# Spreading loads, moving zero rows, and moving three kinds of result stores to Pool's DMA ring in a decode backward kernel

## Chip, cores, metric

One Trainium2 chip, one core. The metric is the device time of one execution in microseconds; smaller is better. An execution can fall into a slower state. A few times by the profiler are quoted from the start of the span; the span is some 1.8 us shorter than the time.

## The reference

The kernel computes the forward result and all gradients of one decode step that adds sliding-window attention over a cache and a GeGLU feed-forward block:

```
xn  = layernorm(x)                                   # x: 4 x 1 x 512
out = x + attention(xn, k_cache, v_cache, wq, wo)    # 32 heads, 8 kv heads, window: last 1024 of 4096 rows
        + (gelu(xn @ w_gate) * (xn @ w_up)) @ w_down # F = 1792
grads of (x, k_cache, v_cache, wq, wo, w_gate, w_up, w_down) for grad_out
```

Two things matter. The gradients of the caches have the full shape 4 x 8 x 4096 x 128, and three quarters of each lie outside the window and are zero: 50.3 MB of zeros must be written. With weights, window and results 112.15 MB are moved.

## The kernel before

The 8 kv heads are worked off in 4 groups of 2 (`t` = 0 to 3). In front of them runs the feed-forward part. Finished results are cast into one pool of four buffers and stored; small pieces of such work stand in a list `bg`, and `tick(n)` takes n of them between other work.

```python
outp = ctx.enter_context(tc.tile_pool(name="outp", bufs=4))     # osb_d, osb_g, osb_o, osb_q all live here
...
    def load_w(t):                                   # weights of a group: 1 MB each
        eng = nc.gpsimd if t else nc.sync            # Pool's ring, except for group 0
        wo_t[t] = pool.tile([P, HG, D], BF16, name="wo_sb", tag="wo")
        eng.dma_start(out=wo_t[t][:], in_=wo_v[t])
        wq_t[t] = pool.tile([P, ND, CW], BF16, name="wq_sb", tag="wq")
        eng.dma_start(out=wq_t[t][:], in_=wq_v[t])
...
    def piece_q(c2, k, held):                        # dwq: rows of 2 KB
        if k == 0:
            held["osb"] = outp.tile([P, 2, GP, rep * Dh], BF16, name="osb_q", tag="o")
...
            store(nc.sync, out=out_4...)
    def piece_d(f4, i, n, held):                     # dWdown: rows of 1 KB
...
            store(nc.sync, out=out_8...)
    def piece_g(s_r, og, c, i, held):                # dWgate, dWup: rows of 3.5 KB
...
            store(nc.sync, out=og...)
...
        load_w(1)                                    # 1 MB + 1 MB
        for k in range(2):
            load_kv(1, k, 1)                         # 1 MB + 1 MB
        for t in range(NT):
...
            odq(t)
            fin(t)
            load_next(t)                             # loads of group t + 2
            tick(len(bg))
            dw(t)
        tick(2)
        zeros(4)                                     # ACT issues zero rows; more stand inside scores()
        tick(len(bg))
        zeros(2 * B * G)
```

So there are three rings, each a queue of transfers that one engine issues: ACT issues zeros (q10), SP issues all results and the loads for the start (q1), and Pool issues loads and nothing else (q0). Pool also makes P_x, the masked attention probabilities, once per group. When the P_x of a group begins tells how far compute has come.

Of the kernel before, what the change touches and what calls it, by code (L numbers as in the profile page):

```python
# [13 lines left out]
BF16 = mybir.dt.bfloat16  # L14
P = 128
# [3 lines left out]
def kernel(  # L19
# [27 lines left out]
    nc = tc.nc  # L47

    B, Sq, D = A_x.shape
# [7 lines left out]
    ND = D // P  # L57
# [4 lines left out]
    NT = G // GP  # L62
    HG = GP * rep
# [5 lines left out]
    CW = HG * Dh  # L69
# [33 lines left out]
    def store(eng, out, in_, kind, apart):  # L103

        d = eng.dma_start(out=out, in_=in_)
        for k in apart:
            tc.declare_no_dep(d.ins, group=k, reason="stores write disjoint parts of the outputs")
        tc.add_to_no_dep_group(kind, d.ins)
        return d
# [6 lines left out]
    for c0 in range(0, NF, NF // 2):  # L116
        nc.sync.dma_start(out=wd_sb[:, c0:c0 + NF // 2, :],
                          in_=B_w_down[c0 * P:(c0 + NF // 2) * P, :].rearrange("(c p) n -> p c n", p=P))
# [47 lines left out]
    for b in range(B):  # L166
        nc.vector.tensor_copy(out=sel[:, :, b * rep:(b + 1) * rep],
                              in_=ident_f[:, b * RB:b * RB + 1].unsqueeze(2).broadcast_to([P, 2 * GP, rep]))
# [69 lines left out]
    for src, dstT, adj in ((dy_b, dyT, False), (xn_b, xnT, True)):  # L238
# [4 lines left out]
        if src is dy_b:  # L243
# [3 lines left out]
                                  in_=tps[:].rearrange("p c (b r) -> p c b r", b=B)[:, :, :, 0:8])  # L247
# [22 lines left out]
    wo_v = A_wo.rearrange("(t p k) n -> t p k n", p=P, k=HG)  # L270
# [5 lines left out]

    loads = deque()

    def load_w(t):
        eng = nc.gpsimd if t else nc.sync  # L280
        pool = wpool[t % 2]
        wo_t[t] = pool.tile([P, HG, D], BF16, name="wo_sb", tag="wo")
        eng.dma_start(out=wo_t[t][:], in_=wo_v[t])
        wq_t[t] = pool.tile([P, ND, CW], BF16, name="wq_sb", tag="wq")
        eng.dma_start(out=wq_t[t][:], in_=wq_v[t])

    def load_kv(t, k, g):
        d_, src, nm = ((k_t, A_k_cache, "kb"), (v_t, A_v_cache, "vb"))[k]
        tl = kvpool[(GP * t + g) % (2 * GP)].tile([P, J, Dh], BF16, name=nm, tag=nm)
        (nc.gpsimd if GP * t + g > GP else nc.sync).dma_start(out=tl[:].rearrange("p j d -> p (j d)"),  # L290
                          in_=src[:, t * GP + g, K0:Sk, :].rearrange("b (m j) d -> m b (j d)", j=J))
        d_[(t, g)] = tl

    def load_next(t):

        if t + 2 < NT:
            load_w(t + 2)
            for k in range(2):
                for g in range(GP):
                    loads.append(lambda k=k, g=g: load_kv(t + 2, k, g))  # L300
# [94 lines left out]
    def scores(t, k, hooks):  # L395

        lf = (qm, dom)[k]
        blks = (k_t, v_t)[k]
        ps = ps_a.tile([P, WQ], FP32, name="S_ps", tag=("S", "dP")[k])
        for g in range(GP):  # L400
            for q in range(NQ):
                T_ps = ps_w.tile([P, JQ, P], BF16, name="T_ps", tag="w")
                for jj in range(JQ):
                    nc.tensor.transpose(T_ps[:, jj, :], blks[(t, g)][:, q * JQ + jj, :], ident[:])  # L404
                T_sb = tsb.tile([P, WQ, B], BF16, name="T_sb", tag="T", bufs=4)
                evac(T_sb[:].rearrange("p n b -> p (n b)"), T_ps[:].rearrange("p j m -> p (j m)"), 1024, half=True)
                s = q * GP + g
                for b in range(B):
                    nc.tensor.matmul(ps[b * RG:(b + 1) * RG, :], lhsT=lf[:, b, s * RG:(s + 1) * RG],  # L409
                                     rhs=T_sb[:, :, b], start=(g == 0 and q == 0),  # L410
                                     stop=(g == GP - 1 and q == NQ - 1), tile_position=(0, b * RG))
                for f in hooks.get(g * NQ + q, ()):
                    f()
                tick(2 if k or q % 2 else 1)
                if q == 1 and loads:
                    loads.popleft()()
                if q == 1:
                    zeros(ZN[t][GP * k + g])
        st[t][("S", "dP")[k]] = ps[:]
# [135 lines left out]
    def dw(t):  # L555

        X = st[t]["X"]

        def piece_o(g, i, held):
            if i == 0:  # L560
                held["osb"] = outp.tile([P, rep, D], BF16, name="osb_o", tag="o")
            mps = ps_w.tile([P, D], FP32, name="dwo_ps", tag="w")
            nc.tensor.matmul(mps[:], lhsT=X[:].rearrange("p h d -> p (h d)")[:, g * rep + i:CW:HG], rhs=dyz[:], start=True, stop=True)  # L563
            evac(held["osb"][:, i, :], mps[:], 512)
            if i == rep - 1:
                store(nc.sync, out=out_5[t * CW:(t + 1) * CW, :].rearrange("(p k) n -> p k n", k=HG)[
                    :, g * rep:(g + 1) * rep, :], in_=held["osb"][:], kind="rest", apart=["zeros", "rest"])

        def piece_q(c2, k, held):
            if k == 0:  # L570
                held["osb"] = outp.tile([P, 2, GP, rep * Dh], BF16, name="osb_q", tag="o")
            ci, g = k // GP, k % GP
            c = c2 * 2 + ci
            mps = ps_w.tile([P, rep * Dh], FP32, name="dwq_ps", tag="w")
            nc.tensor.matmul(mps[:], lhsT=xnz[:, c:D:ND],  # L575
                             rhs=X[:, g * rep:(g + 1) * rep, :].rearrange("p i d -> p (i d)"), start=True, stop=True)
            evac(held["osb"][:, ci, g, :], mps[:], 512)
            if k == 2 * GP - 1:
                store(nc.sync,
                      out=out_4.rearrange("(p c) j -> p c j", c=ND)[:, c2 * 2:(c2 + 1) * 2, t * CW:(t + 1) * CW],  # L580
                      in_=held["osb"][:].rearrange("p c g j -> p c (g j)"), kind="rest", apart=["zeros", "rest"])

        for g in range(GP):
            held = {}
            for i in range(rep):
                bg.append(lambda g=g, i=i, held=held: piece_o(g, i, held))
        for c2 in range(ND // 2):
            held = {}
            for k in range(2 * GP):
                bg.append(lambda c2=c2, k=k, held=held: piece_q(c2, k, held))  # L590
# [24 lines left out]


    NF4 = (NF + 3) // 4
    load_w(0)
    for k in range(2):
        for g in range(GP):  # L620
            load_kv(0, k, g)
# [84 lines left out]
    def piece_d(f4, i, n, held):  # L706
        if i == 0:
            held["osb"] = outp.tile([P, 4, D], BF16, name="osb_d", tag="o")
        mps = ps_w.tile([P, D], FP32, name="dwd_ps", tag="w")
        nc.tensor.matmul(mps[:], lhsT=a_r[:, f4, :], rhs=dym[:, i, :], start=True, stop=True)  # L710
        evac(held["osb"][:, i, :], mps[:], 512)
        if i == n - 1:
            store(nc.sync, out=out_8[4 * f4 * P:(4 * f4 + n) * P, :].rearrange("(h p) n -> p h n", p=P),
                                in_=held["osb"][:, 0:n, :], kind="rest",
                      apart=["zeros", "rest"])

    def piece_g(s_r, og, c, i, held):
        if i == 0:
            held["osb"] = outp.tile([P, NF4, 4, P], BF16, name="osb_g", tag="o")
        n = (NF - i + 3) // 4  # L720
        mps = ps_w.tile([P, NF4, P], FP32, name="dwg_ps", tag="w")
        nc.tensor.matmul(mps[:, 0:n, :].rearrange("p f d -> p (f d)"), lhsT=xnm2[i // 2][:, i % 2, c:D:ND],  # L722
                         rhs=s_r[:, 0:n, :].rearrange("p f d -> p (f d)"), start=True, stop=True)
        evac(held["osb"][:, 0:n, i, :], mps[:, 0:n, :], n * P)
        if i == 3:
            store(nc.sync, out=og.rearrange("(p c) f -> p c f", c=ND)[:, c, :],
                                in_=held["osb"][:].rearrange("p f i d -> p (f i d)")[:, 0:F], kind="rest",
                      apart=["zeros", "rest"])

# [33 lines left out]
    with tc.tile_pool(name="stage", bufs=4, reuse_waits="tile") as stage, \  # L763
            tc.tile_pool(name="wodd", bufs=1, reuse_waits="tile") as wodd:
        wpool.append(wodd)
        kvpool.append(wodd)
        load_w(1)
        for k in range(2):
            load_kv(1, k, 1)
        for t in range(NT):  # L770
            if t == 0:
                pre(t, {})
            masks(t)
            scores(t, 0, {})
            zeros(2 if t == 0 else 0)
            scores(t, 1, softmax(t))
            d1, d2 = softmax_d(t)
            zeros(4 if t == NT - 1 else 0)
            if t + 1 < NT:
                pre(t + 1, {0: [d1], 2: [d2]})  # L780
            else:
                tick(2)
                d1()
                tick(6)
                d2()
                tick(2)
            odq(t)
            fin(t)
            load_next(t)
            tick(len(bg))  # L790
            dw(t)
        tick(2)
        zeros(4)
        tick(len(bg))
        zeros(2 * B * G)

# [65 lines left out]
```

## Time and profile before

| | before |
|---|---|
| time, median of 6 runs | 281.11 us (280.98 to 281.59) |
| span of the profiled run | 279.9 us |
| last vector copy of the result dx | 269.1 us |
| most DMA engines end | 274.7 us |
| last store's last packet | 278.4 us |

The times in the last three rows come from the instruction and packet records. "Most engines end" is the last moment at which at least six of the 16 DMA engines were busy. One more view is needed, the DMA issues: output and input, issuing engine, count, KB of each, and the median time from issue to landing in us.

```profile
out_dram<-osb_q SPq DMA_DIRECT2D x8, 512.0 KB, 13.6
out_dram<-osb_g SPq DMA_DIRECT2D x8, 448.0 KB, 15.8
...
wo_sb<-in_A_wo_dram POOLq DMA_DIRECT2D x3, 1024.0 KB, 11.7
wq_sb<-in_A_wq_dram POOLq DMA_DIRECT2D x3, 1024.0 KB, 21.9
...
out_dram<-osb_d SPq DMA_DIRECT2D x3, 512.0 KB, 9.4
```

The reader is to see that every result store is SP's, and that loads of groups 1 to 3 are Pool's.

### The profile page before, as it was taken

Reading aid. Unit: us, or ns where it says so; the run is one execution under the profiler, and the core shown is the slowest. Engines: PE = TensorE matmul, PEld = TensorE weight load, DVE = VectorE, ACT = ScalarE, POOL = GpSimd, SP = SyncE. Lnnn points to the kernel's source line nnn. Section 1 sums busy time; section 2 is a strip of 40 time slices with the busy share of each in tenths; the row PEclk is TensorE's granted clock in tenths of the full one; section 3 lists DMA queues with packets and bytes.
Section 4 is the critical chain, followed back from the end, with each engine's and each line's share of the span. In section 5 each row is a group of like instructions: output and inputs, shape, how many; then the busy total and the mean of one; then the engine's idle time right before and its main releaser. Section 6 shows DMA issues by size and latency. Waiting matters only on the chain.

```text
span 279.9 us, 7186 instructions
## 1 busy us (share of the span) xinstructions
PE 215.6 (77%) x3126; PEld 140.7 (50%) x3132; DVE 158.9 (57%) x336; ACT 115.3 (41%) x214; POOL 56.0 (20%) x56
## 2 busy tenths in 40 slices
PE   1868986978669869897799897778989769789700
PEld 0856864645346645454466654445665435255300
DVE  6955744645446655563657554547766444577740
ACT  1321733454335245543342553446245435714600
POOL 3890003230200334102001550010142020020000
PEclk9975979899986977997959979999999997898975
DMA  7999999999999999999999999999999999998992
GB/s 233 448 390 429 427 404 393 409 411 417 417 426 427 424 426 409 370 423 422 431 423 419 316 417 423 432 419 427 419 422 393 424 422 421 419 428 351 396 410 114
DMA packets 19440, 112.15 MB, mean 401 GB/s; under 512 B 1473, under 2 KB 5073, under 8 KB 10449
## 3 DMA queue, kind: packets, MB, share of 16 engines
q10 hardware_dynamic: 4416, 50.34, 42.8%
q1 hardware_dynamic: 12304, 44.58, 39.3%
q0 software_dynamic: 2688, 16.78, 15.4%
q8 instruction: 24, 0.39, 0.5%
q14 instruction: 8, 0.06, 0.1%
HBM read 30.68 MB, written 81.01 MB: 399 GB/s over the span
## 4 chain that ended last, share of the span: by engine, by line
PE 56%; DVE 21%; DMA 11%; issue 4%; ACT 2%; POOL 2%; ACTq 0%; DVEq 0%
PE kv_ps L544 11%; PE T_ps L404 9%; DVE T_sb L101 6%; PE S_ps L409 6%; DMA out_dram<-osb_d 6%; DMA out_dram<-osb_g 5%; PE dwo_ps L563 3%; PE acc_ps L213 3%; PE wgT_ps L749 3%; PE wqT_ps L602 3%; PE od_ps L516 3%; PE woT_ps L341 2%; POOL P_x L424 2%; PE pT_ps L435 2%; PE dwq_ps L575 2%
## 5 line engine op out<-in xcount | busy, mean ns | idle before, releaser
L101 DVE COPY T_sb<-T_ps 128x1024 bf16<-128x1024 bf16 x64 | 43.9, 690 | 44.6 <-PE T_ps L404 44.2
L99 ACT CAST stg_dv<-kv_ps 128x512 bf16<-128x512 f32 x57 | 30.4, 592 | 30.4 <-PE kv_ps L544 30.4
L99 ACT CAST stg_dk<-kv_ps 128x512 bf16<-128x512 f32 x40 | 22.2, 588 | 40.3 <-PE kv_ps L544 26.8
L544 PE MATMUL kv_ps<-domr,P_x 128*128 128x512 bf16 x63 | 23.4, 446 | 5.4 <-POOL P_x L424 4.8
L544 PE MATMUL kv_ps<-qmr,dS_x 128*128 128x512 bf16 x60 | 22.3, 459 | 1.8 <-DVE dS_x L424 1.4
L389 POOL TENSOR_TENSOR domr<-r,msk 128x512 bf16<-128x512 bf16 x8 | 8.2, 1040 | 75.1 <-DVE r L382 75.1
L404 PE MATMUL T_ps<-ident,kb 128*128 128x128 bf16 x256 | 22.0, 226 | 0.0
L404 PEld LDWEIGHTS <-kb 128*128 128x128 bf16 x256 | 17.3, 102 | 9.2 <-issue 6.7
L99 ACT CAST osb_g<-dwg_ps 128x512 bf16<-128x512 f32 (+1 forms) x28 | 14.3, 538 | 17.9 <-PE dwg_ps L722 8.0
L404 PE MATMUL T_ps<-ident,vb 128*128 128x128 bf16 x256 | 21.4, 227 | 0.1
L99 ACT CAST osb_o<-dwo_ps 128x512 bf16<-128x512 f32 x25 | 14.6, 586 | 15.3 <-PE dwo_ps L563 14.3
L404 PEld LDWEIGHTS <-vb 128*128 128x128 bf16 x256 | 16.5, 102 | 6.8 <-issue 4.7
L424 POOL TENSOR_TENSOR P_x<-P_b,bmsk 128x1024 bf16<-128x1024 bf16 x4 | 7.6, 1891 | 57.9 <-ACT P_b L472 57.9
L409 PE MATMUL S_ps<-T_sb,dom 128*32 128x256 bf16 x128 | 12.7, 387 | 8.0 <-DVE T_sb L101 7.5
L99 ACT CAST osb_q<-dwq_ps 128x512 bf16<-128x512 f32 x25 | 13.9, 590 | 9.6 <-PE dwq_ps L575 7.5
L101 DVE CAST stg_dk<-kv_ps 128x512 bf16<-128x512 f32 x24 | 16.1, 685 | 2.3 <-PE kv_ps L544 2.2
L409 PE MATMUL S_ps<-T_sb,qm 128*32 128x256 bf16 x128 | 13.1, 389 | 5.1 <-DVE T_sb L101 5.1
L101 DVE COPY woT<-woT_ps 128x1024 bf16<-128x1024 bf16 x16 | 11.0, 689 | 10.2 <-PE woT_ps L341 10.2
L101 DVE COPY wqT<-wqT_ps 128x1024 bf16<-128x1024 bf16 x16 | 11.0, 688 | 6.1 <-PE wqT_ps L602 6.1
L341 PE MATMUL woT_ps<-ident,wo_sb 128*128 128x128 bf16 x128 | 12.3, 249 | 2.7 <-DVE stg_dv L101 1.9
L341 PEld LDWEIGHTS <-wo_sb 128*128 128x128 bf16 x128 | 10.5, 114 | 7.1 <-issue 6.2
L409 PEld LDWEIGHTS <-dom 128*32 128x32 bf16 x128 | 5.3, 93 | 17.5 <-issue 15.7
(214 smaller groups left out, 404.8 us busy)
## 6 DMA issues: line engine op xcount, KB each, us to landing
out_dram<-ztile ACTq DMA_DIRECT2D x13, 3072.0 KB, 19.7
out_dram<-ztile ACTq DMA_DIRECT2D x6, 1536.0 KB, 18.9
out_dram<-stg_dv SPq DMA_DIRECT2D x8, 1024.0 KB, 19.8
out_dram<-stg_dk SPq DMA_DIRECT2D x8, 1024.0 KB, 12.2
kb<-in_A_k_cache_dram POOLq DMA_DIRECT2D x5, 1024.0 KB, 20.4
vb<-in_A_v_cache_dram POOLq DMA_DIRECT2D x5, 1024.0 KB, 25.6
out_dram<-osb_o SPq DMA_DIRECT2D x8, 512.0 KB, 14.5
out_dram<-osb_q SPq DMA_DIRECT2D x8, 512.0 KB, 13.6
```

The source lines that it names most:

```text
L99: last.append(nc.scalar.copy(out=out, in_=in_))
L101: return nc.vector.tensor_copy(out=out, in_=in_)
L213: nc.tensor.matmul(ps[:, c, :], lhsT=lf(c), rhs=rhs, start=(k == 0), stop=(k == len(terms) - 1))
L341: nc.tensor.transpose(wT_ps[:, i, c, :], wo_sb[:, 2 * h2 + i, c * P:(c + 1) * P], ident[:])
L404: nc.tensor.transpose(T_ps[:, jj, :], blks[(t, g)][:, q * JQ + jj, :], ident[:])
L409: nc.tensor.matmul(ps[b * RG:(b + 1) * RG, :], lhsT=lf[:, b, s * RG:(s + 1) * RG], rhs=T_sb[:, :, b], start=(g == 0 and q == 0), stop=(g = ...
L424: eng.tensor_tensor(out=dst[:].rearrange("p j (m b) -> p (j m) b", b=B), in0=src[:].unsqueeze(2).broadcast_to([P, WQ, B]), in1=bmsk[:].uns ...
L516: nc.tensor.matmul(od_ps[r0:r0 + rep * B, 0, :], lhsT=pT[:, j % JQ, (j // JQ) * GP + g:P:NS], rhs=blks[(t, g)][:, j, :], start=(j == 0), s ...
L544: nc.tensor.matmul(mps[:].rearrange("p q d -> p (q d)"), lhsT=src[:, jj, :], rhs=mr[:, g].rearrange("p q d -> p (q d)"), start=True, stop= ...
L563: nc.tensor.matmul(mps[:], lhsT=X[:].rearrange("p h d -> p (h d)")[:, g * rep + i:CW:HG], rhs=dyz[:], start=True, stop=True)
L602: nc.tensor.transpose(wT_ps[:, i, c, :], wq_sb[:, c, h * Dh:(h + 1) * Dh], ident[:])
L749: nc.tensor.transpose(wT_ps[:, i, c, :], wsb[:, c, fc * P:(fc + 1) * P], ident[:])
```

## The change

Its intent: (1) put the loads of a group into a list and pop them one by one, so that they don't burst; (2) let Pool issue the stores of dwq (but for the last group), dWdown, dWgate and dWup, because Pool's ring joins short rows into longer packets (2 KB rows of wq go as packets of 4,096 B, see the prediction); (3) issue some zero rows at the ends of groups, where the DMA engines were idle.

```diff
-    def load_w(t):
+    def load_w(t, k):                  # k = 0: wo, k = 1: wq
...
         if t + 2 < NT:
-            load_w(t + 2)
+            for k in range(2):
+                loads.append(lambda k=k: load_w(t + 2, k))
...
-                if q == 1 and loads:
+                if (q == 1 or (k, q) == (0, 3)) and loads:
                     loads.popleft()()
...
-                store(nc.sync,                                        # osb_q
+                store(nc.gpsimd if t + 1 < NT else nc.sync,
...
-            store(nc.sync, out=out_8[...                              # osb_d
+            store(nc.gpsimd, out=out_8[...
-            store(nc.sync, out=og...                                  # osb_g
+            store(nc.gpsimd, out=og...
...
-        load_w(1)
         for k in range(2):
-            load_kv(1, k, 1)
+            loads.append(lambda k=k: load_w(1, k))
+        for k in range(2):
+            loads.append(lambda k=k: load_kv(1, k, 1))
...
             odq(t)
+            zeros(2 if t == NT - 1 else min(t, 1))
             fin(t)
...
-        zeros(4)
+        zeros(2)
```

More of the change, by code (lines that the diff above doesn't have):

```diff
@@ L277 @@
     loads = deque()
-    def load_w(t):
+    def load_w(t, k):
         eng = nc.gpsimd if t else nc.sync
         pool = wpool[t % 2]
-        wo_t[t] = pool.tile([P, HG, D], BF16, name="wo_sb", tag="wo")
-        eng.dma_start(out=wo_t[t][:], in_=wo_v[t])
-        wq_t[t] = pool.tile([P, ND, CW], BF16, name="wq_sb", tag="wq")
-        eng.dma_start(out=wq_t[t][:], in_=wq_v[t])
+        if k == 0:
+            wo_t[t] = pool.tile([P, HG, D], BF16, name="wo_sb", tag="wo")
+            eng.dma_start(out=wo_t[t][:], in_=wo_v[t])
+        else:
+            wq_t[t] = pool.tile([P, ND, CW], BF16, name="wq_sb", tag="wq")
+            eng.dma_start(out=wq_t[t][:], in_=wq_v[t])
     def load_kv(t, k, g):
@@ L617 @@
     NF4 = (NF + 3) // 4
-    load_w(0)
+    for k in range(2):
+        load_w(0, k)
     for k in range(2):
@@ L712, in piece_d @@
         if i == n - 1:
-            store(nc.sync, out=out_8[4 * f4 * P:(4 * f4 + n) * P, :].rearrange("(h p) n -> p h n", p=P),
+            store(nc.gpsimd, out=out_8[4 * f4 * P:(4 * f4 + n) * P, :].rearrange("(h p) n -> p h n", p=P),
                                 in_=held["osb"][:, 0:n, :], kind="rest",
@@ L725, in piece_g @@
         if i == 3:
-            store(nc.sync, out=og.rearrange("(p c) f -> p c f", c=ND)[:, c, :],
+            store(nc.gpsimd, out=og.rearrange("(p c) f -> p c f", c=ND)[:, c, :],
                                 in_=held["osb"][:].rearrange("p f i d -> p (f i d)")[:, 0:F], kind="rest",
@@ L766 @@
         kvpool.append(wodd)
-        load_w(1)
         for k in range(2):
-            load_kv(1, k, 1)
+            loads.append(lambda k=k: load_w(1, k))
+        for k in range(2):
+            loads.append(lambda k=k: load_kv(1, k, 1))
         for t in range(NT):
```

## The prediction

> **What bounds the kernel now.** I began with the page: its slices, its queues and its chain.
>
> ```profile
> DMA  7999999999999999999999999999999999998992
> GB/s 233 448 390 429 427 404 393 409 411 417 417 426 427 424 426 409 370 423 422 431 423 419 316 417 423 432 419 427 419 422 393 424 422 421 419 428 351 396 410 114
> ...
> q10 hardware_dynamic: 4416, 50.34, 42.8%
> q1 hardware_dynamic: 12304, 44.58, 39.3%
> q0 software_dynamic: 2688, 16.78, 15.4%
> ...
> PE 56%; DVE 21%; DMA 11%; issue 4%; ACT 2%; POOL 2%; ACTq 0%; DVEq 0%
> ```
>
> The reader is to see that the 16 DMA engines are full in 37 of 40 slices. q10 carries the zeros (issued by ACT), q1 what SP issues, q0 what Pool issues; with instruction fetches they add to 98% of the span. The chain of waits names TensorE first, but read in order of time it ends with the last vector copy at 269.1 us; the span ends at 279.9. The last 9 to 10 us are a queue draining. So compute has that much slack and bytes set the end: 112.15 MB at the 420 to 430 GB/s of a good slice would be 261 to 267 us.
>
> Next I cut the time into the stretches where the GB/s line dips, with the busy time of the engines and the DMA share (last two columns):
>
> ```profile
> 154.50:157.00 2.50, 1.77 (x20) 1.26 (x19) 1.38 (x2) 1.57 (x4) 2.48 (x3) 1.00 0.85 298
> 157.00:160.00 3.00, 2.71 (x47) 2.01 (x45) 2.08 (x4) 2.14 (x5) 0.71 (x2) 1.00 0.99 287
> 211.00:213.00 2.00, 2.00 (x23) 1.09 (x20) 1.64 (x3) 1.62 (x4) 1.91 (x2) 1.00 0.78 324
> ...
> 257.00:259.50 2.50, 2.50 (x7) 0.97 (x6) 2.19 (x4) 1.70 (x4) 0.00 (x0) 0.50 0.34 136
> ```
>
> Two kinds of loss are here. Idle engines at the ends of groups: 0.15 x 2.5 + 0.22 x 2 + 0.66 x 2.5 = 2.5 us. And slow packets: at 157 to 160 the share is full but only 287 GB/s move. Third, the last stretch of the queue view:
>
> ```profile
> DMA packets 41, 0.09 MB, mean 18 GB/s; under 512 B 3, under 2 KB 3, under 8 KB 41
> ## 3 DMA queue, kind: packets, MB, share of 16 engines
> q1 hardware_dynamic: 41, 0.09, 4.5%
> ```
>
> That is 274.8 to 279.9 us. 0.045 x 16 x 5.1 us = 3.7 us of engine time, spread over 3.7 us: one engine alone works off its share while 15 have ended. The same lag is in the landings of every late store (15 of 16 completions together, the last 3.8 us later; near 248 us it is 11 us). So the end is set by one lagging engine, not by the mean.
>
> **What the Trainium skill says.** "Perfetto Trace Analysis", section What "DMA-bound" means, lists "specific DMA engines" as one of the things that bind; the lag just shown agrees. "Runtime: NRT & Kernel Launch", Instruction fetch mechanics, says that instructions stream in 16 KiB blocks by DMA; the trace has 24 packets of 16,384 B of some 0.93 us each on q8, 22 us of engine time, enough to make a few engines late, though the records do not name the engine. "DMA: Bandwidth & Descriptors", SWDGE vs HWDGE vs iDMA, gives Pool's packets as 4096 B at best, of up to 64 descriptors. The trace agrees: a wq load has rows of 2 KB, and SP's one goes as 512 packets of 2048 B, each of Pool's three as 256 of 4096 B. The same page, Queues, rings and completion order, says that an engine takes turns between queues packet by packet. The trace agrees: SP's 1 KB packets run at 188 per 0.5 us alone, and at about 10 beside 8 KB packets of Pool and 12 KB packets of zeros.
>
> **The change part by part.** The diff alone misleads here; comparing the order of instructions on each engine, TensorE's order is the same but for two transposes. The scheduler hoists Pool's loads, so of the "spreading" little survives: at the end of group 0, wq moves behind the two qmr multiplies; at the end of group 1, one kb, wo and wq move behind domr or qmr. Worth: near nothing, perhaps 0.3 us in the slow stretches.
>
> *Short rows joined.* What a packet costs:
>
> ```profile
> q1 hardware_dynamic: 753, 0.75, 106.6%
> ...
> q1 hardware_dynamic: 395, 0.79, 101.6%
> ```
>
> The first line is 41.2 to 43.2 us (osb_d, 1 KB rows): 1.066 x 16 x 2 us / 753 = 45 ns. The second is 272.2 to 274.2 us (osb_q, 2 KB): 82 ns. The packet records give medians of 46, 84, 140, 159, 309 and 460 ns for 1, 2, 3.5, 4, 8 and 12 KB: some 9 ns fixed plus bytes at 27 B/ns. Moved to Pool and joined:
> - osb_d, 1792 rows of 1 KB: 1792 x 46 = 82.4 us of engine; as 448 packets of 4 KB, 448 x 159 = 71.2. Over 16 engines 0.70 us saved.
> - osb_q of three groups, 6 stores x 256 rows of 2 KB: 1536 x 84 = 129.0, as 768 x 159 = 122.1: 0.43 us.
> - osb_g, 3.5 KB rows: two do not fit in 4 KB, so I expect nothing.
>
> That is 1.1 us on every engine, the lagging one too. The zeros beside osb_d lose another 0.7 us at 35 to 56 us (12 KB packets over 460 ns); fewer small packets may give back half: 0.35.
>
> *Zeros moved.* One row (0.79 MB, 1.9 us of all engines at 420 GB/s) is now issued at the end of groups 1 and 2 each, and two rows at about 248 instead of four at 258. This puts work exactly where the engines idle: up to 2.5 us of the mean engine. But the lagging engine was 8 us behind at 216 and 11 at 248, so in the gaps at 211 and 257 it was working; it gains only what it idled near 155, at most 0.4 us. This is my main choice: I count 0.3 of the 2.5 us for the end.
>
> *Pool's slow packets.* Against 309 ns, q0's packets lost 3.0 us of 16 engines in total: 1.3 us at 154 to 161 and 0.8 at 112 to 119, where Pool's queue was nearly alone, and almost nothing beside zeros and stores. With a zero row running into 155 I take 0.9 us back; wq after qmr at 112 gains little. The new stores (2,240 packets) may show the same 20 ns extra that Pool's loads average, 2,240 x 20 / 16 = 2.8 us at worst; they run mostly beside zeros, so I take 0.2.
>
> Sum: 1.1 + 0.35 + 0.3 + 0.3 + 0.9 - 0.2 = 2.75 us, and 281.1 - 2.75 is about **278.3 us**.
>
> **Rivals.**
> *The mean engine sets the end.* Then all of 2.5 us idle time counts, and the sum is near 5 us: 276. For it: engines with more backlog could already be caught up by then; against: the single engine at the end.
> *Pool's queue becomes a wait for compute.* Before, ACT waited for buffers of osb in these pieces of the chain:
>
> ```profile
> 42.74 15.72 DMA out_dram<-osb_d
> ...
> 60.67 14.93 DMA out_dram<-osb_g
> ```
>
> Now osb_d no longer starves behind bigger packets, and its last landing should move from 58.5 to about 47. But osb_g stands in Pool's ring behind 4 MB of loads, where on SP it had a ring of its own. From 44 to about 62 us engines move 7.5 MB, 2.9 of it zeros and 4.6 osb_d and loads; then beside zeros Pool gets 8/(8+12) of 420 GB/s, 168, so 0.4 MB of loads and four osb_g (1.8 MB) need 13 us, until 75, which is where the second wait ended before (75.6). P_x also stands behind six osb_g stores on Pool, and behind two osb_q stores later, which before were issued only 1.5 to 1.7 us ahead of it. A delay of 3 us is plausible and vanishes in the 9 us of slack; beyond 7 us it would set the end, 280 to 283.
> *The bytes are hidden anyway.* If the lagging engine's load is mostly fetches and Pool packets, joining still helps it, since each store puts 1/16 on every engine. So no change at all is unlikely.
>
> **Range and chances.** The sure part is 1.1 us, the rest between -1 and +4. So 8 in 10: 275.2 to 280.6. Faster by over 2% needs below 275.5, the mean-engine rival with everything else going well: 0.13. Slower by over 2% needs Pool to stall compute by over 14 us: 0.02. Within 2%: 0.85.
>
> **What would show it.** Joining: q0 holds about 1,200 more 4 KB packets and q1 has 1,792 fewer of 1 KB and 1,536 fewer of 2 KB. Zeros: share 0.95 or more in the slices near 155, 212 and 257, yet a last engine more than 3.8 us behind the others. Pool: q0 packets under 320 ns at the end of group 1. Early phase: the two long DMA waits of the chain still ending near 75 us. Wrong, if the last stretch has no lone engine, if compute ends after the drain, or if q0's packets for the stores are 1 or 2 KB.

## The result

| | before | after |
|---|---|---|
| time, median of 6 runs | 281.11 (280.98 to 281.59) | 283.34 (282.91 to 283.82) |
| span of the profiled run | 279.9 | 281.5 |
| most DMA engines end | 274.7 | 274.2 |
| last store's last packet | 278.4 | 279.6 |
| packet work per engine, at the median of each size, without fetches and 4-byte packets | 266.1 | 264.7 |

The ratio is 1.0077, with a 95% interval of 1.0064 to 1.0090. A ratio is the mean time of one kernel's fast runs over that of the other's in the same rounds, so it isn't quite the ratio of the medians in the table. The change is within 2%, but it is slower, and outside the range of the prediction.

These lines of the page of the changed kernel answer to those of before (slices, queues, chain by engine):

```profile
DMA  7999999999999989999999999999999999999980
GB/s 234 447 392 429 423 420 413 364 404 406 424 406 430 415 356 400 364 420 424 425 426 424 382 403 429 427 419 423 428 426 418 425 429 424 429 424 423 423 327 28
...
q10 hardware_dynamic: 4448, 50.34, 42.7%
q1 hardware_dynamic: 7664, 35.92, 31.1%
q0 software_dynamic: 4704, 25.43, 22.6%
...
PE 45%; DMA 24%; DVE 18%; issue 4%; ACT 3%; POOL 2%; ACTq 0%; DVEq 0%; POOLq 0%
```

q1 lost 12304 - 7664 = 4,640 packets and q0 gained only 2,016: rows were joined. Two dips of before are filled: slice 23 rose from 316 to 382 GB/s, slice 37 from 351 to 423. But slices 15 to 17 (98 to 120 us) now carry 356, 400 and 364 (before 426, 409 and 370), and DMA has risen from 11% to 24% of the chain. The same view of stretches as in the prediction, at the old gaps and at the new ones (DMA share and GB/s are the last two columns):

```profile
98.00:105.00 7.00, 6.40 (x194) 4.77 (x191) 4.48 (x12) 1.90 (x4) 4.08 (x4) 1.00 0.86 347
112.00:119.00 7.00, 6.22 (x64) 3.94 (x61) 4.34 (x7) 3.46 (x6) 3.89 (x5) 0.88 0.96 357
154.50:157.00 2.50, 1.54 (x21) 1.15 (x19) 1.84 (x5) 1.01 (x2) 2.17 (x2) 1.00 1.02 424
...
211.00:213.00 2.00, 2.00 (x63) 1.67 (x61) 0.35 (x2) 0.24 (x1) 0.00 (x0) 0.92 0.99 412
257.00:259.50 2.50, 2.50 (x54) 1.67 (x51) 1.29 (x4) 0.59 (x1) 0.00 (x0) 0.51 0.99 415
```

In the kernel before, the first of these stretches had:

```profile
98.00:105.00 7.00, 4.72 (x37) 3.39 (x38) 3.52 (x7) 2.92 (x6) 2.46 (x3) 0.76 1.01 421
```

The zeros filled the three old gaps (0.85, 0.78 and 0.34 became 0.99 or more), and a new gap opened at 98 to 105 us (by the packet records at 103 to 105). A smaller one opened at 66 to 69; the stretch around it, before and after:

```profile
63.00:70.00 7.00, 5.69 (x60) 3.65 (x61) 3.67 (x10) 3.10 (x8) 0.14 (x1) 1.00 1.02 416
...
63.00:70.00 7.00, 2.84 (x20) 1.29 (x19) 1.14 (x3) 1.55 (x3) 0.44 (x1) 0.50 0.96 400
```

In the chain of waits of the changed kernel (start, duration, what), the two early waits of 15.7 and 14.9 us have become one:

```profile
46.43 19.99 DMA out_dram<-osb_g
```

The landings in the trace tell what it waited behind:

```
issued by Pool     issued   last of 16 engines landed
osb_d (4th)         42.58     52.7
wo, group 1         43.28     56.6
wq, group 1         43.86     59.8
kb, group 1         44.60     62.2
vb, group 1         45.14     65.3
osb_g (1st)         46.43     66.4
```

Each entry of Pool's ring lands after the one ahead of it. The first osb_g store lands 1.2 us after the last of 4 MB of loads, 20.0 us after its issue. The pool of result buffers has four; the cast of the next result waits for that one.

The durations of the chain run from the issue of a store to its landing. How long ACT itself stood still is in the list of waits (us in total, times, longest), two lines of before and one of after:

```profile
ACT osb_g L99 <- DMA out_dram<-osb_g: 6.3, 4, 3.6
ACT osb_g L99 <- DMA out_dram<-osb_d: 3.4, 2, 2.8
...
ACT osb_g L99 <- DMA out_dram<-osb_g: 9.0, 1, 9.0
```

The sum is about the same, but after the change it is one wait, from 57.6 to 66.5 us, and all of it lies before P_x of group 0. Start of P_x, from 69.9 before to 76.9 after (first and last of the four groups):

```profile
L424 POOL TENSOR_TENSOR P_x<-P_b,bmsk x4: 1888/1891/1895, 69.9 to 229.4; 128x1024 bf16<-128x1024 bf16 x4
...
L427 POOL TENSOR_TENSOR P_x<-P_b,bmsk x4: 1882/1882/1887, 76.9 to 233.1; 128x1024 bf16<-128x1024 bf16 x4
```

ACT issues its next zeros in the same stretch, at 66.6 us instead of 61.1, and SP its first store of a cache gradient (stg_dv) at 93.6 instead of 87.3.

### The profile page after: what moved, and what is told of

Read it like the earlier page. It is cut to its first block, busy times and chain, and to the rows that moved or that the text cites. A ratio compares the mean times of both kernels' runs of the same rounds, so it can differ in the third digit from the quotient of the medians.

```text
span 281.5 us, 7191 instructions
## 1 busy us (share of the span) xinstructions
PE 212.4 (75%) x3132; PEld 137.6 (49%) x3132; DVE 159.9 (57%) x336; ACT 115.0 (41%) x214; POOL 67.8 (24%) x74
## 3 DMA queue, kind: packets, MB, share of 16 engines
q1 hardware_dynamic: 7664, 35.92, 31.1%
## 4 chain that ended last, share of the span: by engine, by line
PE 45%; DMA 24%; DVE 18%; issue 4%; ACT 3%; POOL 2%; ACTq 0%; DVEq 0%; POOLq 0%
DMA out_dram<-osb_q 17%; PE kv_ps L547 7%; PE T_ps L407 7%; DMA out_dram<-osb_g 7%; PE S_ps L412 5%; DVE T_sb L101 5%; PE dwo_ps L566 3%; PE wgT_ps L753 3%; PE acc_ps L213 2%; PE woT_ps L344 2%; PE od_ps L519 2%; PE wqT_ps L605 2%; PE dwg_ps L726 2%; POOL P_x L427 1%; ACT osb_q L99 1%
## 5 line engine op out<-in xcount | busy, mean ns | idle before, releaser
L547 PE MATMUL kv_ps<-domr,P_x 128*128 128x512 bf16 x64 | 22.3, 422 | 5.4 <-POOL P_x L427 4.8
L547 PE MATMUL kv_ps<-qmr,dS_x 128*128 128x512 bf16 x64 | 21.2, 408 | 3.0 <-DVE dS_x L427 1.4
L407 PE MATMUL T_ps<-ident,kb 128*128 128x128 bf16 x256 | 22.8, 231 | 0.0
L407 PE MATMUL T_ps<-ident,vb 128*128 128x128 bf16 x256 | 22.3, 233 | 0.0
L99 ACT CAST osb_o<-dwo_ps 128x512 bf16<-128x512 f32 x25 | 14.6, 587 | 16.5 <-PE dwo_ps L566 15.7
L532 POOL TENSOR_TENSOR od_x<-od_r,hmsk 128x1024 bf16<-128x1024 bf16 x4 | 7.6, 1899 | 36.0 <-DVE od_r L523 36.0
L412 PEld LDWEIGHTS <-qm 128*32 128x32 bf16 x128 | 4.4, 93 | 20.6 <-issue 19.1
L566 PE MATMUL dwo_ps<-dyz,od_x 128*128 128x512 bf16 x32 | 14.1, 488 | 0.0
L105 POOL DMA_DIRECT2D out_dram<-osb_q x6 | 4.4, 735 | 39.2 <-ACT osb_q L99 18.7
L101 DVE COPY wgT<-wgT_ps 128x1024 bf16<-128x1024 bf16 x14 | 9.7, 692 | 7.2 <-PE wgT_ps L753 7.2
L344 PE MATMUL woT_ps<-ident,wo_sb 128*128 128x128 bf16 x128 | 11.4, 236 | 2.7 <-DVE stg_dv L101 1.9
## 6 DMA issues: line engine op xcount, KB each, us to landing
out_dram<-ztile ACTq DMA_DIRECT2D x7, 1536.0 KB, 13.3
out_dram<-osb_g POOLq DMA_DIRECT2D x8, 448.0 KB, 10.5
```

What stands on the lines that cost most here:

```text
L99: last.append(nc.scalar.copy(out=out, in_=in_))
L101: return nc.vector.tensor_copy(out=out, in_=in_)
L344: nc.tensor.transpose(wT_ps[:, i, c, :], wo_sb[:, 2 * h2 + i, c * P:(c + 1) * P], ident[:])
L407: nc.tensor.transpose(T_ps[:, jj, :], blks[(t, g)][:, q * JQ + jj, :], ident[:])
L412: nc.tensor.matmul(ps[b * RG:(b + 1) * RG, :], lhsT=lf[:, b, s * RG:(s + 1) * RG], rhs=T_sb[:, :, b], start=(g == 0 and q == 0), stop=(g = ...
L532: nc.gpsimd.tensor_tensor(out=X[:], in0=rows[:].unsqueeze(1).broadcast_to([P, HG, Dh]), in1=hmsk[:].unsqueeze(2).broadcast_to([P, HG, Dh]) ...
```

## The experiments

Theories after the first look. **E (early stall)**: osb_g stands behind the loads of group 1 in Pool's ring; compute is late, ACT issues zeros and SP stores late, and the DMA queues run dry. **Q**: the dwq stores land late in Pool's ring (one issued at 180.23 had its last landing at 229.2). **T (tail)**: at the end SP waited 4.5 and 4.0 us for landings of zeros before it could issue the last dwq store and dx. **Lone engine**: the last DMA engine, made late by instruction fetches, sets the end. Three other quantities from the packet records are used below: the mean idle time of the 16 engines in the stretches 60 to 150 us and 200 to 250 us, and the end of most engines against the last packet.

### One part undone (on the changed kernel)

**a_gsp**, osb_g back on SP:

```diff
-            store(nc.gpsimd, out=og...
+            store(nc.sync, out=og...
```

> The changed kernel with the eight osb_g stores back on SP (osb_d, osb_q on Pool, zeros and loads as changed). Theory E (early stall: osb_g waits in Pool's ring behind 4 MB of loads, a buffer wait of 20 us at 46 us, compute late by some 5 us at 100 us, DMA engines starved at 68 to 70 and 103 to 105 us by 1.3 us in the mean): the stall shrinks to what it was before (two waits of 15 us ending near 75), P_x of group 0 back near 70 us, both dips gone, time 281.3 to 282.0. Theory T (tail: the zeros moved forward leave the end unfilled and SP waits for slow zero landings) and theory Q (osb_q behind loads): time stays at 282.8 to 283.8.

Measured: 283.36 us in the three fast runs (282.24 to 284.29; a fourth, slow one took 286.71), ratio to before 1.0048 (1.0016 to 1.0080). As E says, P_x of group 0 came at 66.6 us (76.9 in the changed kernel) and the idle time of 60 to 150 us fell from 1.68 to 0.00. But the time did not come back. A second wait took its place; TensorE's waits, the chain and the stretch after it:

```profile
PE woT_ps L344 <- DMA wo_sb<-in_A_wo_dram: 13.3, 1, 13.3
...
158.37 38.66 DMA wo_sb<-in_A_wo_dram
...
205.00:217.00 12.00, 9.73 (x228) 6.63 (x226) 8.84 (x18) 4.27 (x9) 3.93 (x3) 1.00 0.60 248
```

Here the load waits behind stores: wo of group 3, issued by Pool at 158.4 us, stands behind dwq stores that Pool issued at 115.6 and 119.5 and that landed at 161 to 168. Its median landing is 183.6, its last 197.0. TensorE waits 13.3 us, and the DMA engines idle 8.6 us between 200 and 250. So the early part of E is shown, but undoing osb_g alone does not answer what it costs.

**a_qsp**, osb_q back on SP:

```diff
-                store(nc.gpsimd if t + 1 < NT else nc.sync,
+                store(nc.sync,
```

> The changed kernel with all osb_q stores back on SP. Theory Q (the osb_q stores of groups 0 to 2 stand in Pool's ring behind up to 3 MB of loads, the second of group 1 landed 49 us after its issue and held a buffer of group 2's pieces at 224 to 229 us; P_x of group 3 is 3.7 us later than before): P_x of group 3 1 to 3 us earlier, time 281.5 to 282.3, in spite of losing 0.43 us of joined rows. E and T: 283.3 to 284.0 (the lost joining, nothing else).

Measured: 283.35 us (281.36 to 285.03), 1.0065 (1.0013 to 1.0116). The runs scatter, but there is no sign of a gain: P_x of group 3, which Q wanted 1 to 3 us earlier, came at 233.8 us (233.1 in the changed kernel). Q is not the cause by itself.

**a_zold**, zeros as before:

```diff
             odq(t)
-            zeros(2 if t == NT - 1 else min(t, 1))
...
-        zeros(2)
+        zeros(4)
```

> The changed kernel with the zeros as before (four rows at 258 us, none at the group ends). Theory T: SP's last store and dx_b no longer wait 4.5 and 4.0 us for slow zero landings, dx_b issued within 1 us of its vector copy, time 281.5 to 282.5. E and Q: the idle of 2 to 2.5 us of the mean engine near 257 returns; if the last engine sets the end, time stays 283.0 to 284.0; if the mean engine does, 285.

Measured: 282.89 us (282.08 to 285.96), 1.0071 (1.0013 to 1.0130). The ratio is that of the changed kernel, so nothing speaks for T. But the edit doesn't settle it: in the profiled run, the slowest of the four, SP still waited 5.2 us for a landing of zeros before the last dwq store. Against T speaks b_z below, where the moved zeros alone cost nothing.

**a_lold**, loads as before:

```diff
-                loads.append(lambda k=k: load_w(t + 2, k))
+                load_w(t + 2, k)
-                if (q == 1 or (k, q) == (0, 3)) and loads:
+                if q == 1 and loads:
-            loads.append(lambda k=k: load_w(1, k))
+            load_w(1, k)
```

> The changed kernel with the loads issued as before (weights together at the group's end, one pop a step). In Pool's order only wq moves ahead of qmr in group 0, and wo/wq ahead of one domr in group 1. All theories E, T, Q: 283.0 to 283.7, within 0.3 us of the changed kernel. If the spreading itself costs time (loads later, DMA engines starved at 112 to 115 us, 0.3 us): 282.6 to 283.0.

Measured: 283.34 us (282.55 to 284.34), 1.0069 (1.0041 to 1.0097). The spreading of loads is neutral.

### One part alone (on the kernel before)

The edits are the matching lines of the change, so they are named only. **b_g**, osb_g on Pool:

> The kernel before with only the eight osb_g stores on Pool. Theory E: the stores stand behind 4 MB of loads, a buffer wait near 20 us, engines starved near 68 and 104 us by over 1 us in the mean: 282 to 283.5. If the ring is not the matter: 281.0 to 281.5 (packets of 7 KB join two rows, worth 0.26 us).

Measured: 285.24 us (283.09 to 286.46), 1.0109 (1.0063 to 1.0156). This part alone costs more than the whole change, and more than the 282 to 283.5 that theory E had named. The chain has the same wait, and the engines ran dry after it (0.70 of the DMA share, and TensorE nearly idle):

```profile
46.88 21.71 DMA out_dram<-osb_g
...
63.00:70.00 7.00, 0.68 (x5) 0.11 (x4) 0.14 (x1) 1.23 (x3) 0.00 (x0) 0.66 0.70 295
```

**b_d**, osb_d on Pool:

> The kernel before with only the four osb_d stores on Pool. Packet work of the mean engine falls by 0.70 us. If joined rows pay wherever they are, and the osb_d stores stand in Pool's ring before the loads: 280.0 to 280.7, 0.4 to 1.1 us below the kernel before. If stores on Pool cost in themselves (Pool's packets slow one engine): 281.5 or more.

Measured: 281.98 us (281.87 to 282.27), 1.0022 (1.0004 to 1.0041). Packet work fell by 0.7 us per engine, as worked out in the prediction. Compute ended 4 us earlier and most engines 2 us earlier, at 272.7, but the last packet stayed at 278.4, the same as before. The time lies in the range that the expectation gave to the rival, that stores on Pool slow one engine; but the kernel before took 281.64 in these rounds, so that range tells little. The rival is not excluded.

**b_q**, osb_q of groups 0 to 2 on Pool:

> The kernel before with only osb_q of groups 0 to 2 on Pool. Theory Q (the stores queue behind loads and hold buffers): 281.7 to 283. If joined rows simply pay: 280.4 to 280.9 (0.43 us of packet work).

Measured: 280.85 us (280.24 to 282.15), 0.9985 (0.9953 to 1.0017). TensorE waited 4.5 us for wq of group 3, and the engines idled 4.0 us between 200 and 250, yet it is not slower.

**b_z**, zeros moved:

> The kernel before with only the zeros moved to the group ends. If the mean engine sets the end: the idle of 2.5 us at 155, 212 and 257 us is filled and the time falls by 1.5 to 2.5 us, to 278.7 to 279.7. If a lone engine sets it: the 15 others end 2 us earlier, the lone one as before, its lag grows from 3.7 to nearly 6 us, time 280.7 to 281.4. If the moved zeros make SP wait for slow landings at the end (theory T): 281.5 to 283.

Measured: 281.00 us (280.83 to 281.76), 0.9989 (0.9969 to 1.0009). Most engines now end at 270.4, 4.3 us earlier than before, and the time stays. The last stretch shows why:

```profile
270.50:278.00 7.50, 0.00 (x0) 0.00 (x0) 0.00 (x0) 0.00 (x0) 0.00 (x0) 0.50 0.07 30
```

0.07 x 16 = 1.1 engines busy over 7.5 us: one engine works alone to 277.8. Filling the gaps helped 15 engines.

**b_l**, loads alone:

> The kernel before with only the loads spread. Pool's order changes at one or two places (wq behind qmr). If harmless: 281.0 to 281.7. If later loads starve the engines or make TensorE wait for weights: 282 or more.

Measured: 281.58 us (281.26 to 281.61), 1.0007 (0.9985 to 1.0028). Neutral.

### What the lone engine is made of

**f_few** is the kernel before with 1,536 TensorE instructions left out. Its results are wrong; the DMA bytes stay but for the instruction fetches. The core of the edit:

```diff
-            for c in range(ND):
+            for c in range(1):
...
-        for j in range(J):
+        for j in range(J // 4):
...
-  ... for k in range(HG)]
+  ... for k in range(2)]
```

> The kernel before with 1,536 fewer instructions on TensorE (a quarter of the steps of the odq products, two of eight terms of the two sums, one of four of do_ps): wrong results on purpose. Bytes, stores and loads are the same. Theory F (the instruction fetches of TensorE, 24 packets of 0.93 us, each holding one DMA engine, make the lone last engine late): 18 packets on q8, the last engine's lag at the end falls from 3.7 us to below 1.5, time 277 to 279. If the lone engine is late for another reason: lag 3 to 4.5 us, time 280.5 to 281.5, although compute ends earlier.

Measured: 278.69 us (277.79 to 280.07), 0.9907 (0.9861 to 0.9952). The fetch queue falls from 24 to 18 packets:

```profile
q8 instruction: 18, 0.29, 0.4%
```

Most engines end at 273.7 and the last at 275.9: the gap falls from 3.7 to 2.2 us, although the engines idled 5.1 us between 200 and 250. That is a little more than the bound I had put on the gap; the time lies where the fetch theory put it.

**a_few** is the same edit on the changed kernel, also wrong.

> The changed kernel with 1,536 TensorE instructions fewer, wrong on purpose. Fetch theory: 18 fetch packets instead of 24, the gap between the end of most engines and the last one falls from about 6 us to under 3.5, and the time is 2 to 3.5 us below the changed kernel's 283.3, so 279.8 to 281.3. Rival, the lone engine has another cause: the gap stays at 5 to 6 us and the time at 282.5 or more.

Measured: 280.10 us (279.48 to 280.86), 0.9974 (0.9947 to 1.0001), 3.2 us under the changed kernel. The gap between most engines and the last falls from 5.4 to 2.4 us (273.3 and 275.7). This fits, but it is not a clean test: with less TensorE work the queues no longer ran dry early either (0.16 us of idle time instead of 1.68 between 60 and 150), in spite of a first osb_g wait of 19.6 us.

In every kernel where I looked, during nearly each fetch packet of some 0.93 us the other queues keep 15.2 engines busy instead of 16.2 (transfers overlap a little, so a full set counts over 16): a fetch takes one engine away. Which engine it is the records do not tell.

**z12 and z8** were to take work off the lone engine: two of the last four zero rows of the kernel before are read from 24 or from 8 partitions, so that only 12 or 8 engines share them. The rule meant in the expectation is that of the Trainium skill, "DMA: Bandwidth & Descriptors", Why a DMA increments its semaphore by 16 and not by 1; that the lowest-numbered engines are taken is the page's word, no run here shows it.

> The kernel before with two of the last four rows of zeros written from 24 instead of 64 partitions, so that by the skill's rule 12 of the 16 DMA engines carry them, the lowest-numbered. If the lone last engine is one of the upper four it is spared 3.7 us: lag gone, time 278.7 to 279.7 (the twelve others get 1.2 us more). If it is one of the lower twelve: it gets 1.2 us more, time 282.0 to 282.8. If a lone engine does not set the end: 281.0 to 281.6.

> As before, with the two rows written from 8 partitions, so by 8 engines, the lowest-numbered. These get 3.7 us more, the upper eight 3.7 us less. If the lone engine is one of the upper eight: lower ones now end last, near 278.5, time 281 to 281.8, with eight engines at the end instead of one. If it is one of the lower eight: it ends near 282, time 284 to 285.

Measured: 286.23 us (285.99 to 288.51), 1.0193, and 304.07 us (303.80 to 304.44), 1.0809. The counts of 12 and 8 busy engines are in the records, but the 8 KB packets read from so few partitions took 641 and 1,251 ns instead of 309. That cost drowned the question; the tests say nothing on the lone engine.

### The place in Pool's ring

**e_swap** is the changed kernel with the loads of group 1 issued by SP, so that osb_g has nothing ahead of it but osb_d:

```diff
-        eng = nc.gpsimd if t else nc.sync
+        eng = nc.gpsimd if t > 1 else nc.sync
...
-        (nc.gpsimd if GP * t + g > GP else nc.sync).dma_start(
+        (nc.gpsimd if GP * t + g > GP + 1 else nc.sync).dma_start(
```

> The changed kernel with the loads of group 1 (wo, wq, kb, vb of the second head) issued by SP and no longer by Pool, so that osb_g stands behind nothing but osb_d in Pool's ring. Place-in-the-ring theory: the first osb_g store lands within 8 us of its issue (20.0 us in the changed kernel), the third softmax-gradient product P_x of group 0 ends before 71 us (76.9), the engines do not run empty at 68 to 70 and 103 to 105 us, the 7,168 B packets stay, and the time is 278.5 to 281. Rival, Pool's ring as such is slow for these stores: the first store still needs 15 us or more and the time is 282.5 to 284. A third outcome: early compute is repaired as in a_gsp, but a weight of group 3 comes late behind dwq stores in Pool's ring, TensorE waits over 5 us for it between 200 and 215 us, and the time is 282 to 284.

Measured: 286.52 us (285.32 to 287.36), 1.0198 (1.0161 to 1.0235). The third outcome, and worse than named. The early stall is gone: the first osb_g store landed 10.7 us after its issue (20.0 in the changed kernel, 8 expected), P_x came at 67.9, and the early gaps are closed. But Pool's ring still holds dwq stores ahead of the weights of group 3:

```profile
PE woT_ps L344 <- DMA wo_sb<-in_A_wo_dram: 13.5, 1, 13.5
...
157.17 41.22 DMA wo_sb<-in_A_wo_dram
...
205.00:217.00 12.00, 9.68 (x241) 6.44 (x240) 8.95 (x17) 3.79 (x7) 3.49 (x3) 1.00 0.61 249
```

**e_swap2** takes this conflict out as well: as e_swap, with the dwq stores on SP and the loads popped as before. Pool still issues osb_d and osb_g.

> As e_swap, with the dwq stores back on SP and the loads popped as in the kernel before; so Pool's ring has osb_d, osb_g and the loads of groups 2 and 3 only. Place-in-the-ring theory: P_x of group 0 ends before 71 us, no weight of group 3 comes late (TensorE waits under 2 us for wo), time 278.5 to 280.5. Rival, Pool's ring as such: 282.5 to 284.

Measured: 281.35 us (280.79 to 281.81), 1.0018 (0.9995 to 1.0042). The first store landed after 10.5 us, P_x came at 67.3, TensorE did not wait for wo or wq of group 3 (last landings at 176.5 and 168.0), and the stretch that had run dry is full:

```profile
63.00:70.00 7.00, 5.09 (x54) 3.32 (x55) 3.38 (x7) 3.97 (x9) 2.96 (x3) 1.00 1.03 431
```

The time is above the range by 0.85 us: nothing is gained, which I put down to the lone engine; but the loss is gone. Against b_g (1.0109) the difference is the loads ahead of osb_g and parts that cost about 0.2% or less (b_d, b_z, b_zd). So the loss comes from the place in the ring, and not from Pool's ring as such.

**b_zq**, zeros moved and osb_q on Pool, the two parts that had been under 1 alone:

> The kernel before with two parts of the change only: zeros moved, dwq stores of groups 0 to 2 on Pool. If their effects add (b_z 0.9989, b_q 0.9985): ratio 0.997, 280.3 to 280.9. If the late weight of b_q (TensorE waits 4 us or more for wq near 200 us) is worse with zeros in the way: 281.5 to 283.

Measured: 283.05 us (281.80 to 283.48), 1.0070 (1.0043 to 1.0098). They don't add; the second outcome holds. In the profiled run, which was the fastest of the four by 1.1 us, TensorE waited 5.7 us for wo of group 3; what made the other three slower has no trace.

**b_zd**, zeros moved and osb_d on Pool, what is left of the change when both ring conflicts are out:

> The kernel before with two parts of the change only: zeros moved, dWdown stores (osb_d) on Pool. No ring conflict is left (osb_g and dwq on SP). Lone-engine theory: most engines end near 269 to 271 us, the last one at 277 to 278.5 as in b_z and b_d, and the time is within 0.3% of before, 280.3 to 282. Rival, the saved 0.7 us and the filled gaps reach the end once the conflicts are gone: 278.0 to 279.8.

Measured: 281.58 us (281.43 to 281.76), 1.0011 (0.9980 to 1.0041). The last packet came at 278.0 and the time is that of before, as the lone engine says. Most engines ended at 275.6 and not near 270, a miss: they idled 4.8 us between 200 and 217, for which I found no single wait.

### All runs side by side

Idle times are means over 16 engines, in us; the last two columns are the end of most engines and of the last store's packets. They are those of each kernel's one profiled run, which is not always a typical one: it was the fastest in b_zq and the slowest in a_zold, a_lold and b_g. z12 and z8 are left out.

| kernel | ratio to before | idle 60-150 | idle 200-250 | most end | last |
|---|---|---|---|---|---|
| before | 1 | 0.08 | 0.43 | 274.7 | 278.4 |
| b_z | 0.9989 | 0.00 | 0.02 | 270.4 | 277.8 |
| b_q | 0.9985 | 0.00 | 4.03 | 276.8 | 278.1 |
| b_l | 1.0007 | 0.00 | 0.47 | 272.4 | 278.3 |
| b_zd | 1.0011 | 0.00 | 4.84 | 275.6 | 278.0 |
| e_swap2 | 1.0018 | 0.00 | 3.20 | 275.1 | 278.0 |
| b_d | 1.0022 | 0.00 | 0.09 | 272.7 | 278.4 |
| b_zq | 1.0070 | 0.18 | 3.75 | 275.0 | 278.3 |
| after | 1.0077 | 1.68 | 0.00 | 274.2 | 279.6 |
| a_qsp | 1.0065 | 1.30 | 0.37 | 274.7 | 279.7 |
| a_lold | 1.0069 | 1.09 | 0.08 | 274.5 | 280.6 |
| a_zold | 1.0071 | 1.75 | 0.08 | 276.5 | 282.1 |
| b_g | 1.0109 | 3.22 | 0.00 | 277.7 | 283.2 |
| a_gsp | 1.0048 | 0.00 | 8.64 | 279.9 | 281.0 |
| e_swap | 1.0198 | 0.00 | 9.00 | 281.3 | 281.9 |
| f_few | 0.9907 | 0.00 | 5.14 | 273.7 | 275.9 |
| a_few | 0.9974 | 0.16 | 0.32 | 273.3 | 275.7 |

The table reads in three blocks. Where the engines did not run dry before 150 us, the last packet comes at 277.8 to 278.4, whatever most engines did (270.4 to 276.8) and with up to 4.8 us of late idle time. Where they ran dry early, it comes at 279.6 or later. Where they idled 8.6 us or more late, it comes at 281.0 or later, and then most engines end close to it. Only the two kernels with fewer fetches, and less compute, came under 277. The ratio of b_zq (1.0070) is out of line with its last packet, for its other three runs were slower than the profiled one.

It stays open why an early gap goes with a later end and one of 5 us near 210 does not. One could think that the lone engine falls behind gradually and so has no backlog to work on in an early gap. The landings do not bear that out. In the kernel before, the last of 16 landings came 2.6 us after the median for a load issued at 106.4 us, but already 9.3 us for the next, issued at 106.9; then 6.9 us for one issued at 160.7 and 3.8 us for the last stores. In the middle of the kernel several of the 16 are late, not one: 4 of 16 by 5.9 to 10.6 us for a store issued at 238.4.

## Why the prediction was wrong

**Joined rows: right in size, worth nothing at the end.** Packet work fell by 1.39 us per engine (1.13 predicted). The 0.26 us more is osb_g: the prediction said two rows of 3.5 KB do not fit in 4 KB, and the trace has 512 packets of 7,168 B, two rows each. But of the 1.1 us credited to "every engine, the lagging one too", b_d shows none at the lone engine: 278.4 before and with it.

**Zeros: right.** The three gaps are filled, and the lone engine stayed later than 3.8 us behind the others (5.4). The main choice, that the lone engine and not the mean sets the end, is shown by b_z. What the prediction read from the landings, "15 of 16 completions together", holds for stores issued from 258 us on only; earlier several were late, as told above.

**Slow packets: right in place, lost elsewhere.** The 0.9 us credited to Pool's packets did come where it was seen: at 154 to 161 us their time over the median of each size fell from 1.3 to 0.3 us per engine (the 8 KB packets there still took 417 ns, not under 320). But at 42 to 70 us, in the middle of which Pool had the engines nearly to itself during ACT's wait, it grew from 0.4 to 0.7, and at 161 to 168 from 0.1 to 0.4. In total only 0.3 us remained (3.05 to 2.75). The 0.35 us for the zeros beside osb_d did not come: over the whole span the loss of zero packets rose from 1.70 to 2.31.

**Loads: right.** Neutral in b_l and a_lold.

**The step that failed** is the rival "Pool's queue becomes a wait for compute", which was sized as vanishing. Its mechanism was named rightly: osb_g behind 4 MB of loads. What was wrong is the event that was watched. The prediction compared the end of the second wait (75.6 before, 75 worked out) and found no delay. Four osb_g had in fact landed even sooner, by 69.7, for the sum counted zeros beside them that ACT, itself waiting, had not yet issued. But in the kernel before P_x of group 0 came at 69.9, ahead of the end of the second wait, so it can't have hung on that; it hangs on what comes before. P_x follows the end of the first wait, or the landing of the first osb_g store, by 9.7 to 11.4 us in these kernels (in e_swap and e_swap2 ACT had no need to wait for that store: its next cast came at 58.9 and 58.2 us, released by TensorE):

| kernel | first wait ends, or first osb_g landed | P_x, group 0 |
|---|---|---|
| before | 58.5 (wait for osb_d) | 69.9 |
| after | 66.4 | 76.9 |
| b_g | 68.6 | 79.1 |
| e_swap | 58.2 | 67.9 |
| e_swap2 | 57.3 | 67.3 |

So compute was 7.0 us late, which is just the bound that the prediction had set ("beyond 7 us it would set the end, 280 to 283"). It did not set the end in the way written there: dx was ready at 270.9 (269.1 before), before most engines ended. The second mistake is the word slack. That compute ended later did no harm by itself, but compute issues the zeros and produces the stores, so a delay of 7 us emptied the queues at 66 to 69 and 103 to 105 us (with smaller gaps 1.68 us of idle time against 0.08). The last packet came 1.2 us later in the profiled runs; that the idle time is what delayed the lone engine is inferred from the table above. The tail from there to the end of the span is 0.4 us longer (1.9 against 1.5), and the profiled run of before took 281.66 us, 0.55 more than its median, that of after 283.35, which is its median; together these are the 2.2 us between the medians.

**What stays open.** Which DMA engine is the lone one, and whether fetches alone make it late (f_few and a_few remove compute work together with fetches) or Pool's stores add to it (b_d). Why early idle time reaches the end and late idle time does not. No version with right results beats the kernel before by more than its interval: b_q and b_z are at 0.9985 and 0.9989, with intervals that include 1.

## What to carry to other kernels

In every run here the transfers of Pool's ring landed in the order of their issue. Before a store or a load is moved to another ring, list what it will stand behind there: a store behind 4 MB of loads kept a buffer busy for 20 us, and a load behind stores was late for the next stage by up to 13.5 us. The first alone cost 3 us (b_g), twice the 1.4 us of packet work that joining rows saved; the second alone cost nothing (b_q), but 5.6 us in e_swap. Taking out one of the two conflicts may only expose the other (a_gsp, e_swap). Loads and stores in one ring are not bad as such: b_d and e_swap2 have both in Pool's and lost 0.2%. When a wait is moved, ask which of the old waits the next stage hung on, and follow that one; and when compute has slack, ask what it issues, since a late issuer leaves the queues empty. In the profiled runs 1.1 us or more of such idle time before 150 us went with a later last packet, while up to 4.8 us between 200 and 250 did not.

## What the Trainium skill lacked or had wrong

- "DMA: Bandwidth & Descriptors", SWDGE vs HWDGE vs iDMA, gives a packet as 4096 B preferably. The runs show 512 packets of 7,168 B (two rows of 3.5 KB) from Pool's ring, at 272 ns each, against 140 ns for one row of 3.5 KB. Here I took a preference for a limit, though the trace of before already had 1,664 packets of 8,192 B from Pool's ring.
- The same page, Two DMAs through the same engine are not ordered, says that descriptors of one queue start in order. "Perfetto Trace Analysis", DMA Optimizations, comes near: it advises one issuing engine for inputs and another for outputs, but neither page says that a transfer stands behind what its ring already holds nor what that costs. The runs show it: a store 4 MB deep in a ring landed after 20.0 us, with nothing but short stores ahead of it after 10.5 us; weights behind dwq stores made TensorE wait up to 13.5 us.
- "Runtime: NRT & Kernel Launch", Instruction fetch mechanics, calls the cost of crossing a block boundary "mostly hidden". In a kernel bound by DMA a block takes one of 16 engines for 0.93 us, 22.7 us of engine time in all; six blocks fewer went with 1.5 to 3.0 us less of a gap at the last engine (with less compute work at the same time, as told above).
- "DMA: Bandwidth & Descriptors", Latency and other measured facts, says that DMA engines 7 and 15 are usually slower than the others. The runs show a single engine that ends up to 7.4 us after the rest (b_z); the records do not name it, so the page is neither confirmed nor refuted.
